# A written-out instruction order with a new tail: transformer block on one core, TensorE's groups reordered from the 167th on

## The chip, the core and the metric

The kernel runs on one core of one Trainium2 chip. The core has five engines that take instructions from queues of their own and wait for each other through semaphores: TensorE (PE in the profile; its weight loads are listed apart as PEld), VectorE (DVE), ScalarE (ACT), GpSimd (POOL) and SyncE (SP), which here only issues transfers. Transfers run on 16 DMA engines. The metric is the device time of one execution in microseconds (us), and one profiled execution gives the trace.

## The reference

The inputs are one sequence of 2048 tokens with 512 features (bfloat16), a condition vector and the weights. What has to come out is a transformer block whose two layer norms and two residual adds are modulated by the condition:

```python
mod = (silu(c) @ w_mod).reshape(1, 6, 1, -1)           # sa, ca, ga, sb, cb, gb
h = layernorm(x) * (1 + ca) + sa
x = x + ga * attention(h, wqkv, wo)     # 32 heads of 16; 8 keys: own position, -2, -4, ... -14
h = layernorm(x) * (1 + cb) + sb
x = x + gb * ((silu(h @ w1) * (h @ w3)) @ w2)          # 512 -> 1792 -> 512
```

A query sees its own position and the seven at distances 2 to 14 behind it, so attention has no square matrix: it is eight elementwise products of q with a shifted k, a softmax over eight numbers, and eight products with a shifted v.

## The kernel before

**Tiles and stages.** The 2048 tokens are 16 tiles T of 128 tokens. After layer norm 1, TensorE makes q, k and v (L691, L711). Per tile, VectorE multiplies q with eight shifted views of k in one instruction (L742, `pq`), and TensorE sums the products per head with a matrix of ones (L752, `lg`). The softmax runs on VectorE and ScalarE (L764 to L797, the exponential at L782), TensorE turns the weights (L807, `at`) and ScalarE copies them out (L811). Four transfers fetch eight shifted views of v for a tile (`vl`), VectorE multiplies them with the weights (L827, `av`), TensorE adds them up (L855, `ac`), ScalarE copies the sum to SBUF (L861), a transposing transfer turns it (L124, tile `ot`), TensorE multiplies with `wo` (L867, `wo`), and VectorE adds the result to x and takes its row sum (L871, `rs`).

**Layer norm 2.** For a pair of tiles GpSimd makes minus the mean from the two row sums (L586). ScalarE squares (L590, twice). GpSimd makes the reciprocal deviation and the bias in three small instructions (L596, L597, L599). ScalarE then normalises both tiles (L601). For the second group of tiles on, a transposing transfer per tile and four modulating ScalarE instructions (L621) make the `h` that the feed-forward part reads.

**Feed-forward part.** Tiles go through it in six groups: 0-1, 2-3, 4-7, 8-11, 12-13, 14-15. A group has 14 blocks of 128 hidden features. A block is four TensorE matmuls with w1 (the gate) and four with w3 (the up), both L883, 256 or 512 tokens wide. ScalarE takes the silu of the gate (L889), and VectorE multiplies it with the up (L892). The matmuls with w2 (L921, `z`) come in two halves of seven per tile, and VectorE adds x and the result is stored (L931).

**What sets the order.** No compiler orders anything here. `_build` makes 1118 operations with their dependencies; the list `ORDER` gives the sequence in which they are put into the queues of their engines, and `SLOTS` gives each pooled buffer its place (eight PSUM banks, six silu buffers, 20 product buffers and more). `synchronize` adds the waits that dependencies and buffer reuse need. An engine works through its queue strictly in order: an instruction that waits holds up all that stand behind it. A PE entry of the list is a group of matmuls, for example the four of one gate.

The numbers of `ORDER` that the text below uses:

- tiles 4 to 7: 470 is `ac` of tile 7, 471 its copy, 472 its transposing transfer, 473 its `wo`; 460 is `ac` of tile 6 and 459 its `av`; 746 is the gate of block 26, 733 a product of block 22; 484 is the last softmax step (L797) of tiles 8-9; 509 and 507 are `pq` of tiles 11 and 10; 767 is L599 of tiles 4-5 on GpSimd, 769 and 768 are the two L601 behind it; 773 to 775 are L596 to L599 of tiles 6-7; 717, 701, 719 and 721 are the products of blocks 18 and 14 and the silu and product of block 19; 753, 737 and 749 are products of blocks 27, 23 and 26; 501 and 491 are `av` of tiles 9 and 8
- tiles 8 to 11: 496 and 506 are `rs` of tiles 8 and 9, 858 is L586 of the two on GpSimd, 859 the first L590 behind it; 533 and 523 are `av` of tiles 11 and 10; 534 and 524 are their `ac`, 535 and 525 the copies; 833 and 821 are products of blocks 39 and 36
- tiles 12 to 15: 565 and 575 are `wo` of tiles 12 and 13, 566 and 576 their `rs`, 954 is L586 of the two, 956 and 955 the two L590; 586 and 596 are `av` of tiles 14 and 15, 587 and 597 their `ac`, 588 and 598 the copies, 590 and 600 their `wo`; 886 and 887 are gate and silu of block 43; 843, 847 and 851 are second halves of `z` (seven matmuls each)

Of the kernel before, what the change touches and what calls it, by code (L numbers as in the profile page):

```python
# [272 lines left out]
def _build(p, A_x, A_wqkv, A_wo, B_w1, B_w3, B_w2, c, w_mod, out):  # L273
# [722 lines left out]
    316, 444, 405, 406, 319, 617, 622, 626, 407, 446, 627, 395, 396, 397, 419, 420, 623, 477, 45, 634, 635, 447, 642, 618, 272, 320,  # L996
    46, 636, 637, 628, 629, 619, 620, 621, 52, 226, 326, 51, 630, 631, 408, 624, 625, 344, 638, 448, 421, 422, 50, 640, 639, 641,
    662, 670, 644, 643, 645, 449, 409, 646, 410, 450, 632, 647, 47, 633, 654, 398, 399, 451, 663, 666, 400, 671, 672, 452, 48, 343,
    650, 655, 668, 667, 669, 648, 649, 682, 683, 684, 453, 652, 651, 653, 435, 656, 657, 664, 433, 436, 685, 454, 665, 673, 658,
    678, 434, 437, 321, 426, 686, 687, 689, 695, 688, 694, 691, 660, 323, 659, 661, 423, 478, 475, 696, 424, 438, 425, 697, 690,  # L1000
    692, 674, 693, 742, 439, 730, 465, 731, 466, 468, 743, 427, 744, 745, 726, 706, 708, 707, 709, 476, 479, 467, 469, 428, 458,
    429, 710, 711, 456, 457, 712, 713, 722, 723, 724, 727, 728, 729, 455, 732, 733, 440, 725, 430, 746, 698, 699, 459, 53, 702, 703,
    480, 54, 470, 471, 472, 734, 735, 441, 442, 460, 461, 345, 346, 714, 431, 432, 738, 762, 462, 481, 497, 482, 473, 474, 483, 675,
    676, 747, 763, 463, 464, 704, 498, 484, 764, 765, 499, 715, 487, 716, 717, 700, 701, 718, 720, 509, 770, 771, 679, 705, 750,
    736, 737, 490, 748, 772, 485, 719, 500, 749, 488, 721, 739, 740, 752, 741, 507, 766, 767, 769, 489, 779, 768, 751, 754, 753,
    486, 501, 773, 774, 778, 775, 776, 780, 777, 781, 782, 491, 785, 758, 759, 760, 327, 783, 755, 529, 502, 510, 508, 492, 784,
    798, 818, 511, 512, 503, 531, 532, 680, 830, 493, 513, 330, 530, 831, 521, 539, 832, 514, 515, 820, 822, 814, 799, 815, 522,
    819, 504, 505, 516, 517, 541, 494, 324, 520, 495, 518, 506, 834, 806, 786, 807, 496, 761, 836, 794, 833, 823, 835, 677, 821,
    838, 858, 808, 859, 681, 533, 534, 559, 519, 523, 535, 809, 837, 540, 558, 542, 543, 524, 860, 525, 570, 790, 796, 795, 788,
    797, 545, 861, 791, 810, 787, 789, 802, 792, 793, 526, 544, 536, 547, 546, 549, 548, 862, 537, 569, 538, 550, 803, 527, 528,  # L1010
    839, 863, 864, 804, 805, 811, 551, 594, 812, 813, 866, 824, 825, 867, 800, 567, 593, 552, 553, 554, 874, 592, 868, 869, 826,
    557, 816, 560, 801, 840, 827, 870, 871, 555, 872, 568, 556, 817, 876, 841, 865, 854, 875, 561, 873, 846, 877, 828, 571, 842,
    595, 881, 562, 572, 829, 577, 563, 584, 855, 879, 578, 579, 564, 573, 850, 856, 580, 574, 878, 880, 906, 908, 581, 596, 565,
    566, 575, 576, 954, 857, 585, 907, 583, 909, 918, 919, 894, 582, 586, 843, 956, 955, 957, 886, 887, 958, 756, 898, 587, 588,
    895, 597, 890, 891, 589, 926, 847, 598, 599, 959, 960, 962, 899, 900, 901, 927, 961, 848, 590, 600, 591, 601, 1032, 910, 920,
    921, 963, 964, 965, 892, 893, 967, 966, 1034, 928, 1033, 1035, 1036, 1037, 851, 968, 852, 849, 972, 974, 976, 978, 973, 980,
    929, 911, 984, 986, 977, 979, 975, 844, 845, 985, 987, 853, 1039, 988, 990, 989, 1038, 930, 931, 932, 981, 982, 983, 933, 902,
    904, 991, 903, 905, 970, 934, 969, 1040, 896, 897, 971, 882, 1041, 888, 889, 884, 883, 922, 885, 923, 935, 936, 924, 946, 1043,
    1042, 942, 937, 938, 950, 1004, 1006, 1005, 1007, 1000, 1045, 1002, 1001, 925, 1008, 1012, 1009, 1013, 1016, 1017, 996, 998,
    997, 914, 999, 915, 1018, 992, 1003, 1044, 993, 994, 1014, 1015, 1019, 995, 916, 757, 912, 917, 1024, 913, 939, 1028, 940, 1070,  # L1020
    1090, 1071, 1086, 1072, 1073, 1091, 1010, 1087, 1074, 1011, 1082, 1075, 1088, 941, 1083, 1078, 1089, 1079, 1092, 1093, 1094,
    1084, 1096, 1095, 1097, 1080, 1081, 943, 951, 1085, 952, 944, 947, 948, 949, 1054, 1050, 1066, 1051, 1052, 1053, 953, 945, 1020,
    1062, 1064, 1076, 1077, 1063, 1046, 1067, 1068, 1069, 1047, 1055, 1056, 1057, 1021, 1022, 1023, 1058, 1060, 1059, 1061, 1029,
    1048, 1025, 1098, 1049, 1030, 1065, 1099, 1100, 1101, 1110, 1111, 1112, 1114, 1115, 1113, 1116, 1117, 1026, 1027, 1102, 1031,
    1103, 1104, 1105, 1106, 1107, 1108, 1109,
]
SLOTS = [
    7, 0, 1, 2, 3, 4, 5, 6, 0, 1, 2, 3, 4, 5, 6, 7, 0, 1, 2, 3, 4, 5, 6, 7, 0, 3, 4, 5, 6, 0, 1, 1, 0, 2, 3, 0, 4, 0, 7, 1, 0, 2, 1,
    2, 3, 6, 1, 5, 0, 7, 5, 7, 6, 2, 2, 1, 4, 0, 1, 3, 1, 2, 0, 4, 1, 4, 0, 7, 5, 1, 3, 6, 3, 0, 4, 2, 0, 1, 2, 1, 1, 0, 2, 4, 0, 1,
    2, 1, 4, 3, 6, 5, 1, 1, 0, 1, 3, 2, 3, 2, 4, 0, 0, 2, 3, 4, 1, 0, 3, 5, 6, 5, 1, 5, 3, 3, 2, 2, 0, 2, 6, 1, 2, 0, 3, 6, 7, 5, 3,  # L1030
    0, 1, 1, 0, 6, 0, 1, 1, 0, 0, 0, 0, 0, 1, 1, 5, 1, 6, 0, 1, 1, 1, 0, 5, 1, 0, 3, 1, 5, 0, 2, 3, 1, 4, 0, 2, 4, 2, 100, 5, 1, 2,
    5, 1, 1, 0, 1, 4, 0, 7, 1, 0, 4, 0, 1, 1, 1, 1, 5, 0, 7, 0, 0, 1, 1, 6, 0, 1, 1, 1, 0, 5, 1, 0, 0, 100, 7, 0, 2, 1, 1, 6, 0, 2,
    6, 2, 100, 5, 1, 1, 3, 1, 3, 0, 2, 5, 0, 4, 1, 0, 0, 1, 0, 1, 6, 0, 0, 6, 1, 0, 4, 1, 7, 0, 2, 6, 6, 1, 0, 0, 1, 1, 6, 100, 2,
    0, 0, 2, 1, 4, 7, 2, 1, 5, 103, 2, 102, 3, 101, 6, 103, 1, 100, 4, 101, 5, 104, 2, 106, 4, 102, 3, 100, 3, 105, 2, 104, 1, 102,
    4, 105, 1, 100, 3, 108, 5, 104, 2, 109, 4, 105, 7, 110, 5, 102, 7, 113, 5, 103, 6, 111, 2, 102, 6, 107, 6, 101, 1, 112, 0, 100,
    3, 102, 0, 3, 2, 0, 4, 4, 104, 0, 101, 1, 105, 1, 102, 1, 105, 7, 115, 1, 103, 4, 116, 7, 100, 2, 100, 5, 101, 7, 105, 7, 101,
    5, 119, 2, 102, 1, 117, 7, 100, 7, 118, 5, 103, 2, 103, 4, 100, 5, 106, 5, 104, 4, 114, 2, 102, 0, 104, 6, 104, 4, 107, 2, 101,
    0, 101, 2, 1, 4, 3, 1, 1, 105, 5, 113, 3, 100, 1, 100, 6, 101, 0, 112, 1, 103, 5, 115, 3, 101, 1, 101, 6, 100, 5, 110, 6, 100,
    7, 102, 0, 102, 1, 116, 4, 101, 5, 109, 3, 104, 6, 105, 3, 101, 5, 103, 0, 105, 7, 108, 4, 105, 0, 111, 7, 105, 7, 119, 1, 103,
    3, 100, 5, 102, 4, 103, 0, 1, 2, 4, 2, 3, 105, 5, 108, 6, 103, 7, 105, 6, 105, 4, 114, 4, 102, 1, 115, 7, 101, 4, 106, 7, 100,  # L1040
    4, 113, 7, 100, 0, 104, 7, 104, 1, 114, 1, 100, 4, 113, 7, 104, 0, 107, 6, 100, 1, 116, 0, 100, 3, 117, 0, 101, 3, 110, 2, 102,
    4, 109, 7, 100, 3, 102, 0, 101, 5, 103, 0, 3, 0, 6, 101, 0, 103, 2, 101, 0, 100, 4, 105, 5, 118, 2, 100, 1, 102, 3, 100, 7, 101,
    4, 105, 5, 112, 4, 103, 6, 108, 2, 100, 4, 119, 4, 103, 6, 104, 6, 101, 2, 111, 2, 105, 1, 100, 4, 102, 1, 105, 1, 101, 2, 106,
    3, 103, 0, 113, 2, 102, 6, 100, 1, 2, 1, 0, 102, 3, 116, 1, 103, 5, 118, 4, 104, 5, 110, 7, 100, 4, 114, 0, 101, 1, 117, 7, 105,
    7, 109, 4, 102, 4, 115, 7, 100, 5, 107, 7, 102, 1, 108, 4, 104, 7, 112, 7, 103, 1, 101, 1, 101, 4, 102, 1, 105, 4, 103, 5, 105,
    0, 100, 3, 101, 6, 103, 7, 101, 4, 103,
]


# [26 lines left out]
```

## Time and profile before

| | |
|---|---|
| three runs | 239.98, 240.88 and 242.07 us, median 240.88 |
| the profiled execution | 240.36 us, of which 238.6 us are the span of its instructions |
| TensorE | busy 232.2 us (97% of the span), 1806 matmuls |
| VectorE | busy 179.4 us (75%) |
| ScalarE | busy 138.3 us (58%) |
| GpSimd | busy 28.8 us (12%) |
| granted TensorE clock | 1.0 throughout |
| transfers | 38.85 MB |

How to read the views quoted below: the timeline has start, duration, engine, line, operation, tiles and count, and in brackets the idle time ahead of the instruction with what ended it. The chain of waits has start, duration and what ran, over the instructions that lead back from the last one. A matmul's duration is its latency; matmuls overlap, so their pace is read from starts. The table of stages has, for each stretch, its length and the busy time and count of each engine.

### The profile page before, as it was taken

How to read it: one execution, taken by the hardware profiler on the slowest of the kernel's cores; microseconds unless marked ns; L12 is line 12 of the kernel's file. 1: busy time of each engine (PE TensorE's matmuls, PEld its weight loads, DVE VectorE, ACT ScalarE, POOL GpSimd, SP SyncE). 2: the span in 40 equal slices, each digit the busy share in tenths (PEclk: the TensorE clock that was granted, in tenths of full speed). 3: DMA queues.
4: the chain of work that ended last, by engine and by line, in shares of the span. 5: the costliest groups of instructions: out<-in, count | busy, mean ns of one | idle time of the engine just before them, and what ended most of it. 6: DMA issues, size and time to landing. Idle time of an engine off the chain costs nothing.

```text
span 238.6 us, 4560 instructions
## 1 busy us (share of the span) xinstructions
PE 232.2 (97%) x1806; PEld 136.7 (57%) x1806; DVE 179.4 (75%) x279; ACT 138.3 (58%) x267; POOL 28.8 (12%) x66
## 2 busy tenths in 40 slices
PE   7999999999999998999999999999899999999995
PEld 4776554545688683664444444444375457485874
DVE  5699999999999999899999999690653403434433
ACT  2289587899978737776765594747553406040300
POOL 4434000013002000240003420020010000000000
PEclk9999999999999999999999999999999999999999
DMA  6999999999999996876972783634303000000202
GB/s 216 372 330 309 157 242 301 217 288 315 302 293 254 247 203 178 240 180 193 229 220 62 192 209 76 166 113 46 67 5 104 3 0 0 3 22 0 69 1 88
DMA packets 46317, 38.85 MB, mean 163 GB/s; under 512 B 21704, under 2 KB 37080, under 8 KB 46296
## 3 DMA queue, kind: packets, MB, share of 16 engines
q1 hardware_dynamic: 46288, 38.56, 65.1%
q8 instruction: 14, 0.23, 0.4%
q14 instruction: 7, 0.06, 0.1%
q10 hardware_dynamic: 8, 0.00, 0.0%
HBM read 29.62 MB, written 4.21 MB: 142 GB/s over the span
## 4 chain that ended last, share of the span: by engine, by line
PE 83%; DMA 8%; DVE 3%; SPq 3%; ACT 1%; issue 0%
PE pall L883 40%; PE pall L921 17%; PE pall L691 7%; PE pall L867 5%; DMA sb_x<-in_A_x_dram 5%; PE pall L711 4%; DMA sb_ot<-sb_ac 3%; PE pall L752 3%; SPq L124 3%; PE pall L855 3%; PE pall L909 3%; DVE sb_pq L742 2%; DVE sb_st L555 1%; PE pall L807 1%; DVE sb_xn L576 1%; ACT sb_ac L861 0%
## 5 line engine op out<-in xcount | busy, mean ns | idle before, releaser
L883 PE MATMUL pall<-sb_h,sb_w 128*128 128x256 bf16 (+1 forms) x672 | 102.6, 308 | 0.0
L883 PEld LDWEIGHTS pall<-sb_h,sb_w 128*128 128x128 bf16 x672 | 65.0, 98 | 35.7 <-issue 2.5
L889 ACT ACTIVATE sb_sg<-pall 128x256 bf16<-128x256 f32 (+1 forms) x84 | 35.6, 454 | 54.5 <-PE pall L883 53.4
L892 DVE TENSOR_TENSOR sb_hh<-sb_sg,pall 128x256 bf16<-128x256 bf16 (+1 forms) x84 | 40.0, 505 | 36.1 <-PE pall L883 34.0
L921 PE MATMUL pall<-sb_w,sb_hh 128*128 128x512 bf16 x196 | 44.9, 379 | 0.0
L742 DVE TENSOR_TENSOR sb_pq<-sb_q,sb_kT 128x4096 bf16<-128x4096 bf16 x16 | 36.3, 2282 | 0.0
L921 PEld LDWEIGHTS pall<-sb_w,sb_hh 128*128 128x128 bf16 x196 | 19.0, 98 | 21.6 <-DVE sb_hh L892 0.4
L691 PE MATMUL pall<-sb_h,sb_wqkv 128*128 128x512 bf16 (+1 forms) x160 | 31.0, 336 | 0.0
L827 DVE TENSOR_TENSOR sb_vsh<-sb_vsh,sb_al 128x4096 bf16<-128x4096 bf16 x12 | 27.2, 2284 | 0.5 <-DMA sb_vsh<-v_scratch_dram 0.5
L621 ACT ACTIVATE sb_h<-sb_h,sb_modc 128x512 bf16<-128x512 bf16 (+1 forms) x24 | 16.5, 743 | 9.1 <-DMA sb_h<-sb_xn 9.1
L691 PEld LDWEIGHTS pall<-sb_h,sb_wqkv 128*128 128x128 bf16 x160 | 14.7, 98 | 11.7 <-ACT sb_ac L861 0.4
L931 DVE TENSOR_TENSOR sb_o<-pall,sb_x 128x512 bf16<-128x512 f32 (+1 forms) x18 | 11.1, 628 | 10.9 <-PE pall L921 7.1
L867 PE MATMUL pall<-sb_wo,sb_ot 128*128 128x512 bf16 x64 | 16.0, 379 | 1.9 <-DMA sb_ot<-sb_ac 1.9
L711 PE MATMUL pall<-sb_wqkv,sb_h 128*128 128x512 bf16 x64 | 16.0, 379 | 0.0
L644 ACT ACTIVATE sb_h<-pall,sb_modc 128x256 bf16<-128x256 bf16 (+1 forms) x18 | 9.9, 611 | 7.9 <-DVE sb_modc L509 6.9
L586 POOL TENSOR_SCALAR sb_nm<-sb_sx 128x2 f32<-128x2 f32 x8 | 1.7, 218 | 105.3 <-DVE sb_x L871 105.3
L861 ACT ACTIVATE sb_ac<-pall 128x512 bf16<-128x512 f32 x16 | 9.5, 595 | 7.1 <-PE pall L855 6.9
L601 ACT ACTIVATE sb_xn<-sb_x,sb_nb,sb_rs 128x512 bf16<-128x512 bf16 x16 | 12.4, 807 | 0.7 <-POOL sb_nb L599 0.6
L871 DVE SCALAR_TENSOR_TENSOR sb_x<-pall,sb_x 128x512 bf16<-128x512 f32 x16 | 10.8, 686 | 2.2 <-PE pall L867 2.1
L590 ACT ACTIVATE sb_xn<-sb_x,sb_nm 128x512 bf16<-128x512 bf16 x16 | 11.4, 714 | 1.8 <-POOL sb_nm L586 1.8
L721 ACT ACTIVATE sb_v<-pall 128x512 bf16<-128x512 f32 x16 | 9.6, 605 | 2.8 <-PE pall L711 2.8
L555 DVE BATCH_NORM_STATS2 sb_st<-sb_x 128x6 f32<-128x512 bf16 x16 | 10.5, 679 | 0.7 <-DMA sb_x<-in_A_x_dram 0.6
(87 smaller groups left out, 209.5 us busy)
## 6 DMA issues: line engine op xcount, KB each, us to landing
sb_vsh<-v_scratch_dram SPq DMA_DIRECT2D x48, 256.0 KB, 5.2
sb_vshx<-v_scratch_dram SPq DMA_DIRECT2D x16, 256.0 KB, 4.4
sb_w<-in_B_w_dram SPq DMA_DIRECT2D x6, 512.0 KB, 7.6
sb_w<-in_B_w_dram SPq DMA_DIRECT2D x6, 384.0 KB, 4.2
v_scratch_dram<-sb_v SPq DMA_DIRECT2D x16, 128.0 KB, 6.1
out_dram<-sb_o SPq DMA_DIRECT2D x14, 128.0 KB, 1.8
sb_wqkv<-in_A_wqkv_dram SPq DMA_DIRECT2D x6, 256.0 KB, 6.3
sb_x<-in_A_x_dram SPq DMA_DIRECT2D x4, 256.0 KB, 6.5
```

Source lines behind the costliest of these rows:

```text
L555: o = p.op("dve", lambda e, T=T: e.bn_stats(st[:, T, :], x_sb[:, T, :]), 595, ("st", T), r=[vx[T]], w=[vs])
L601: p.op("act", lambda e, vn=vn, T=T: e.activation(vn.at[:], x_sb[:, T, :], ACT.Identity, bias=nb[:, T, :], scale=rs[:, NT + T, :]), c_act(5 ...
L621: return e.activation(vh.at[:, ft, 0:n * P], vh.at[:, ft, 0:n * P], ACT.Identity, bias=modc[:, 8 * which + ft:8 * which + ft + 1], scale=m ...
L691: ins = e.matmul(bank(vp)[:, j * n:(j + 1) * n], wqkv[:, t, col:col + P], vh.at[:, t, 0:n], start=(t == ORDER[0] and j == 0), stop=(t == O ...
L711: ins = e.matmul(bank(vp), vh.at[:, t, tt * P:(tt + 1) * P], wqkv[:, t, 2 * D:3 * D], start=(t == ORDER[0]), stop=(t == ORDER[-1]))
L742: return e.tensor_tensor(vp.at[:], in0, in1, ALU.mult)
L827: return e.tensor_tensor(v_w, v_w, a_w, ALU.mult)
L867: ins = e.matmul(bank(vy), vt.at[:, ft, :], wo[:, ft, :], start=(ft == 0), stop=(ft == KT - 1))
L883: ins = e.matmul(bank(vp)[:, 0:n], wt[:, t, fi * P:(fi + 1) * P], vh.at[:, t, 0:n], start=(t == 0), stop=(t == KT - 1))
L889: p.op("act", lambda e: e.activation(vt.at[:, 0:n], bank(vgp)[:, 0:n], ACT.Silu), c_act(n), k, r=[vgp], w=[vt], table="silu")
L892: p.op("dve", lambda e: e.tensor_tensor(vh_.at[:, 0:n], vt.at[:, 0:n], bank(vup)[:, 0:n], ALU.mult), c_dve(n), k, r=[vt, vup], w=[vh_])
L921: ins = e.matmul(bank(vz), vhh[fi].at[:, tt * P:(tt + 1) * P], w2[:, fi, :], start=(fi == 0), stop=(fi == NF - 1))
```

## The change

Only the two lists change. TensorE gets the same groups from its 167th on in another sequence, with the silus, products, copies and adds that belong to them; the buffers are assigned anew (314 of 655 places). The queues of GpSimd and of the transfers keep their order, apart from the order of the last output stores. No instruction is added or taken away. The rewritten part of `ORDER` begins so:

```diff
-    650, 655, 668, 667, 669, 648, 649, 682, 683, 684, 453, 652, 651, 653, 435, 656, 657, 664, 433, 436, 685, 454, 665, 673, 658,
-    678, 434, 437, 321, 426, 686, 687, 689, 695, 688, 694, 691, 660, 323, 659, 661, 423, 478, 475, 696, 424, 438, 425, 697, 690,
+    650, 655, 668, 667, 669, 648, 649, 682, 683, 684, 453, 652, 651, 653, 435, 656, 657, 664, 433, 436, 685, 454, 434, 321, 426,
+    423, 424, 425, 678, 658, 686, 687, 688, 690, 694, 689, 465, 466, 468, 691, 467, 665, 673, 437, 695, 323, 660, 478, 659, 661,
...
```

Sorted by engine, these are the places that the prediction speaks of (old line, then new line):

```
TensorE, 184th to 201st group
- 428 710 712 722 724 728 732 746 698 702 470 734 441 460 714 431 738 473
+ 730 726 734 710 724 712 728 732 702 470 441 714 698 460 746 431 738 473
VectorE, around `av` of tile 6 (459) and the products of blocks 14 to 27
- 729 733 725 459 480 442
+ 725 729 459 480 733 442
- 484 717 701 509 705 737 749 721 741 507 753 501 491
+ 484 509 717 705 701 741 721 507 753 737 749 501 491
ScalarE, same place
- 771 772 719 739 769 768 751 486 776 777
+ 771 772 739 769 768 719 776 777 751 486
VectorE, tiles 8 to 11
- 541 506 496 833 821 533 523
+ 541 833 506 533 821 496 523
ScalarE, same place
- 835 859 535 860 525 795
+ 835 859 535 860 795 525
VectorE, tiles 12 to 15
- 596 566 576 909 586 756
+ 596 576 909 566 586 756
ScalarE, same place
- 907 919 956 955 887 588 895 891 598 960
+ 907 956 955 887 588 598 960
TensorE, from the 272nd group
- 906 908 565 575 918 894 843 886 898 587 597 890 926 847 900 590 600 910
+ 898 851 575 906 908 565 843 886 926 587 597 847 928 890 892 590 922 900 600 924
```

The waits that the new lists give at three of these places: 524 (`ac` of tile 10) waits for 535, the copy of tile 11's sum, and for 523; 597 (`ac` of tile 15) waits for 887, the silu of block 43; 954 (GpSimd) waits for 566.

## The prediction

> **What bounds the kernel now.** I read the busy shares first, then the waits of TensorE alone, then the table of stages.
>
> ```profile
> PE 232.2 (97%) x1806; PEld 136.7 (57%) x1806; DVE 179.4 (75%) x279; ACT 138.3 (58%) x267; POOL 28.8 (12%) x66
> ...
> PE pall L867 <- DMA sb_ot<-sb_ac: 1.9, 2, 1.0
> ...
> 96.00:152.00 56.00, 56.00 (x405) 27.89 (x404) 54.34 (x68) 37.90 (x68) 9.99 (x15) 1.00 0.70 181
> ...
> 170.00:238.60 68.60, 65.99 (x445) 43.21 (x442) 25.85 (x54) 20.53 (x49) 1.30 (x4) 1.00 0.09 26
> ```
>
> PE is busy 97% of the span. Over the new part of the order (76 us to the end) it waits three times: twice for a turned tile `ot`, and once for an `av` (the row of 92.04 below). Between 96 and 152 us it never stops, but VectorE is busy 54.34 of those 56.00 us, so whatever VectorE delays there has no spare time to be made up in. The number of PE groups does not change; so the new order can win only those three waits, and lose only by new ones.
>
> The sizes of the two waits for `ot`, by the PE timeline and the chain of waits:
>
> ```profile
> 93.90 0.60 PE L883 MATMUL pall<-sb_h,sb_w 128*128 128x256 bf16 x4
> 95.54 1.02 PE L867 MATMUL pall<-sb_wo,sb_ot 128*128 128x512 bf16 x4 [1.04 <-DMA sb_ot<-sb_ac]
> ...
> 166.51 1.03 PE L867 MATMUL pall<-sb_wo,sb_ot 128*128 128x512 bf16 x4
> 168.35 1.04 PE L867 MATMUL pall<-sb_wo,sb_ot 128*128 128x512 bf16 x4 [0.81 <-DMA sb_ot<-sb_ac]
> ...
> 90.82 1.03 PE L867 MATMUL pall<-sb_wo,sb_ot 128*128 128x512 bf16 x4
> 92.04 0.61 PE L855 MATMUL pall<-sb_vsh,sb_ind 128*32 128x512 bf16 x8 [0.19 <-DVE sb_vsh L827]
> ...
> 91.12 4.29 DMA sb_ot<-sb_ac
> ...
> 98.08 0.86 PE pall L867 x4
> 98.94 2.18 PE pall L883 x20
> 101.12 1.51 PE pall L921 x7
> ```
>
> Matmuls overlap, so I count from start to start, as the chain does: four matmuls of 512 columns take 0.86, seven 1.51, and four of 256 take 2.18 / 5 = 0.44. Hence `wo` of tile 7 is late by 95.54 - 93.90 - 0.44 = 1.20, `wo` of tile 15 by 168.35 - 166.51 - 0.86 = 0.98, `ac` of tile 6 by 92.04 - 90.82 - 0.86 = 0.36. Together 2.54 us: the most that can be won.
>
> **The change part by part.** I went through the new order group by group and put each under the time that its releaser had in this trace. From 76.7 to 89 us groups only trade places and every releaser is early enough: 0 (0 to 0.2 lost).
>
> *Tiles 6 and 7 (89 to 96 us).* The gate 746 (0.44) moves behind `ac` of tile 6, and the product 733 behind `av` of tile 6. So `av` starts earlier, and of 0.36 about 0.07 is left; `ac` of tile 7 and the transfer 472 behind it come 0.44 earlier, issued at 90.68. When it lands is the question. The DMA view for 90.5 to 95.5 us (each digit 0.125 us) and the tile view of `sb_ot`:
>
> ```profile
> DMA  9999999999600029996700000000000059994000
> ...
> q8 instruction: 1, 0.02, 1.7%
> ...
> DMA to landing us min/median/max: 2.4/3.6/6.6
> ```
>
> Most of the transfer is over at 93.4 us (digit 24 on is 0), and nothing else runs until the next transfer; the landing is counted at 95.41, after one block of PE's own instructions went through a DMA engine (1.7% of 16 engines' 5 us is 1.3 us on one). I read the late landing as this block in front of one sixteenth of the transfer. PE fetches it by its place in its own program, which in the new order comes 0.25 to 0.5 us earlier, so it may meet the transfer again. End A: same landing time, 90.68 + 4.29 + 0.13 = 95.10, 0.44 gained. End B: the shortest landing, 90.68 + 2.4 = 93.1, no wait at all, and `wo` of tile 7 starts at 94.05, 1.49 gained.
>
> The Trainium skill, "Runtime: NRT & Kernel Launch", section "Instruction fetch mechanics", says that crossing a 16 KiB instruction boundary is mostly hidden. By that alone end B would hold; this trace shows a landing of 4.29 against a shortest of 2.4, so here the fetch is not hidden from a waiting transfer.
>
> *GpSimd behind VectorE.* The next three parts rest on one observation, GpSimd's timeline beside VectorE's:
>
> ```profile
> 100.72 0.20 POOL L599 TENSOR_TENSOR sb_nb<-sb_nm,sb_rs 128x2 f32<-128x2 f32 x1
> 101.62 1.58 POOL L596 TENSOR_SCALAR sb_rs<-sb_var 128x2 f32<-128x2 f32 x1 [0.70 <-ACT sb_xn L590]
> ...
> 122.20 0.22 POOL L586 TENSOR_SCALAR sb_nm<-sb_sx 128x2 f32<-128x2 f32 x1 [17.95 <-DVE sb_x L871]
> 129.06 2.10 POOL L596 TENSOR_SCALAR sb_rs<-sb_var 128x2 f32<-128x2 f32 x1 [6.64 <-ACT sb_xn L590]
> 131.24 0.70 POOL L597 TENSOR_TENSOR sb_rs<-sb_rs,sb_cst 128x2 f32<-128x2 f32 x1
> ```
>
> ```profile
> 100.20 0.74 DVE L892 TENSOR_TENSOR sb_hh<-sb_sg,pall 128x256 bf16<-128x256 bf16 x2
> 100.86 2.29 DVE L742 TENSOR_TENSOR sb_pq<-sb_q,sb_kT 128x4096 bf16<-128x4096 bf16 x1
> ...
> 122.02 0.08 DVE L871 DVE_READ_ACCUMULATOR sb_x<-pall,sb_x 128x1 f32 x1
> ...
> 125.42 2.29 DVE L827 TENSOR_TENSOR sb_vshx<-sb_vshx,sb_al 128x4096 bf16<-128x4096 bf16 x1
> 128.82 2.28 DVE L742 TENSOR_TENSOR sb_pq<-sb_q,sb_kT 128x4096 bf16<-128x4096 bf16 x1
> 131.62 2.28 DVE L742 TENSOR_TENSOR sb_pq<-sb_q,sb_kT 128x4096 bf16<-128x4096 bf16 x1
> ...
> 156.57 0.69 DVE L871 SCALAR_TENSOR_TENSOR sb_x<-pall,sb_x 128x512 bf16<-128x512 f32 x1
> ```
>
> The small GpSimd instruction that starts within a `pq` or `av` ends with it: 101.62 + 1.58 = 103.20 beside 100.86 + 2.29 = 103.15; 129.06 + 2.10 = 131.16 beside 128.82 + 2.28 = 131.10. One that starts ahead keeps its length: L599 at 100.72, 0.14 ahead of its `pq`, took 0.20; L597 at 131.24 took 0.70 and ran 0.32 into the `pq` of 131.62, which took 2.28 all the same.
>
> The Trainium skill, "SBUF — State Buffer", section "Who interferes with whom", has this as a rule: a VectorE instruction with two SBUF inputs contends with a GpSimd instruction that reads SBUF, and the one that issues first blocks the other for its whole length. The held GpSimd rows agree; the `pq` of 131.62, not lengthened, does not show the other half. By the full rule a `pq` behind a GpSimd start would lose at most 0.3 here.
>
> *Tiles 8 and 9's `av` (96 to 113 us).* `pq` of tile 11 stands directly behind 484, two products (100.20 to 100.86, 0.33 each) no longer ahead of it: it starts about 100.2, and 767 (the L599 of 100.72) falls inside it and ends near 102.4 instead of 100.92, 1.5 later. Behind 767 waits the L601 pair, and in the new order the silu 719 waits behind that pair:
>
> ```profile
> 101.44 0.63 ACT L889 ACTIVATE sb_sg<-pall 128x256 bf16<-128x256 f32 x2
> 101.97 1.51 ACT L601 ACTIVATE sb_xn<-sb_x,sb_nb,sb_rs 128x512 bf16<-128x512 bf16 x2
> 124.25 0.73 ACT L590 ACTIVATE sb_xn<-sb_x,sb_nm 128x512 bf16<-128x512 bf16 x1
> 127.68 0.60 ACT L861 ACTIVATE sb_ac<-pall 128x512 bf16<-128x512 f32 x1 [2.60 <-PE pall L855]
> 160.67 0.60 ACT L889 ACTIVATE sb_sg<-pall 128x512 bf16<-128x512 f32 x1 [1.24 <-PE pall L883]
> ...
> 104.88 6.21 PE L921 MATMUL pall<-sb_w,sb_hh 128*128 128x512 bf16 x28
> 128.36 0.61 PE L855 MATMUL pall<-sb_vshx,sb_ind 128*32 128x512 bf16 x8
> ...
> 156.36 1.89 PE L883 MATMUL pall<-sb_h,sb_w 128*128 128x512 bf16 x8
> 158.09 1.67 PE L921 MATMUL pall<-sb_w,sb_hh 128*128 128x512 bf16 x7
> 161.86 0.60 PE L855 MATMUL pall<-sb_vshx,sb_ind 128*32 128x512 bf16 x8
> ```
>
> Pair from 102.5 to 104.0, silu to 104.3 (two took 101.44 to 101.97), its product 721 to 104.75 with the handing over, `pq` of tile 10 to 106.95, three products to 107.95; then the third `z` of the 28, which before began at 104.88 + 2 x 1.51 = 107.90, can begin. In end A PE stood 0.44 ahead, and this uses it up. In end B the whole chain starts earlier with PE, and I estimate that 0.9 to 1.0 of the 1.49 stays. Call what is kept d: 0 to 1.0.
>
> *`ac` of tile 10 (120 to 130 us).* VectorE's six pieces ahead of `av` of tile 10 are the same (end 127.71 - d), but 496, the last row sum, now stands directly ahead of that `av`. The L586 of 122.20 needs it, so it starts inside the `av` and ends at 127.77 - d. Behind it is the L590 (0.71) at 127.82, and behind that the copy of tile 11's sum (0.60), until 129.13 - d. PE's `ac` of tile 10 waits for that copy: 129.2 - d against 128.36. With respect to before PE is then late by L = 0.85 - d. In end B that is below nothing.
>
> *`ac` of tile 15 (152 to 165 us).* The new order has a `z` half (1.51) where a group of 0.86 stood: +0.65 that comes back later. 565 is last ahead of the `z` that was at 158.09, which now begins at 158.74 + L. Its row sum 566 starts 0.21 behind the group's end, as the one of 156.57 did behind 156.36, and ends at 159.65 + L; `av` of tile 14 stands directly behind and takes until 161.86 + L; the L586 954 is held inside it to 161.92; two L590 follow (0.71 each, to 163.39), then the silu 887 (0.60, to 163.99), and `ac` of tile 15 waits for 887: 164.09 + L. PE would be there at 161.86 + 0.65 + L = 162.51 + L. A new wait of 1.58.
>
> *`wo` of tile 15.* Its 0.98 goes: two more groups stand ahead, and from `ac` of tile 15 to it are 7.2 us (one 1.51, six 0.86, 0.54). The two copies behind `ac` end near 165.4 + L; even with 4.29 the tile lands at 169.7 + L, and PE needs it at 171.3 + L. This cover ends only at a landing of 5.9.
>
> Behind 170 us VectorE is busy 25.85 of 68.60 us and ScalarE 20.53, so a silu or product that moves has room, and the tail of the list has the same dependencies: 0.
>
> Sum: L + 1.58 - 0.98 = 1.45 - d, with d from 0 to 1.0: **+0.45 to +1.45** on the profiled execution's 240.36, 240.8 to 241.8. That execution is 0.52 below the median of 240.88, so 241.3 to 242.3 as a median. I take the middle of d, since nothing in the trace tells where the block falls: +0.95, **241.8**.
>
> **The rivals.**
>
> *GpSimd is first (not slower).* The two held L586 are the price. In the trace L586 started at 122.20, 0.10 behind the end of the row sum's last piece (122.02 + 0.08); VectorE's pieces follow each other without a gap, so the hold should come; but if `av` loaded 0.2 us later, L586 would run in 0.22 as before, the copy would be at its old 127.7, and silu 887 done at about 161.9, ahead of PE. Then neither 0.85 nor 1.58 is paid and 0.98 + 0.44 to 0.98 + 1.49 is won: 237.9 to 238.9, or 238.4 to 239.5 as a median. For it speak the rows of 100.72 and 131.24, which were first by 0.14 and 0.38; against it, the order of the list. 0.14.
>
> *A second block of instructions on a transposition that PE waits for (slower).* The page has 14 such blocks of PE in 238.6 us, one per 17 us. `wo` of tile 8 now goes before that of tile 9, and the last transpositions of the layer norm stand closer to their groups. The price is 4.29 - 2.4 = 1.9, of which the two new waits could cover some: 1.0 to 1.9, 241.8 to 243.3 on the profile's base, 242.3 to 243.8 as a median. It decides if a block begins within the 2.4 us of a transfer that has under 1.9 us to spare: 2.4 / 17 = 0.14 for each. 0.16.
>
> ```profile
> q8 instruction: 14, 0.23, 0.4%
> ```
>
> *Only names move.* If releasers were early everywhere (no hold, no late copy, no better `ot`), the time would stay at 240.9. VectorE's 54.34 of 56.00 us speaks against it. 0.08.
>
> **How the numbers follow.** Forecast 0.56, the rivals 0.14, 0.16 and 0.08, 0.06 for what I don't see. 1%, about what a measurement of this kernel can tell from no change, is 238.47 to 243.29. Faster by more: the lower edge of the first rival and half of the unseen, 0.06. Slower by more: the upper third of the second and some of the unseen, 0.10. The rest, 0.84, is within. The range from 239.3 to 243.3 holds the forecast, the third rival and most of the second; it leaves out nearly all of the first.
>
> **What would show it.** Right: the GpSimd row of L586 near 125 and 160 us lasts about 2.2 us instead of 0.22; PE waits at L855 near 128 and 163 us, released by ScalarE; no wait of PE at L867 near 171 us; L599 near 100 us lasts over 1.5 us. The wait at L867 near 95 us gives d. Wrong: short L586 rows with no wait at L855 (then the first rival), a landing above 4 us ahead of other `wo` (the second), or a wait behind 170 us, which I have at nothing.

## The result, and the profile after

The changed kernel takes 241.72 us (median of 22 runs) and the kernel before 240.00 us (median of 22 runs, the three shown above among them). The ratio is 1.0084, 95% interval 1.0061 to 1.0107: slower by 0.8%, clear of the noise, and of a size that the prediction put within 1%. Two slow runs of the changed kernel (247.72 and 851.74 us) are left out of the ratio, and the two medians alone give 1.0072. The profiled execution took 241.0 us with a span of 239.3, so the two traces differ by 0.7 us only, the medians by 1.7. That gap is part of what had to be explained.

The waits of PE behind 76 us, changed kernel (what PE waited for, us in total, times, longest), where before had the two `ot` and an `av`:

```profile
PE pall L855 <- ACT sb_sg L889: 1.3, 1, 1.3
PE pall L855 <- ACT sb_ac L861: 0.8, 1, 0.8
```

The three old waits are gone and two new ones stand at `ac`. Some matmul records are missing in this trace (1779 of 1806), so I read starts and not sums. The PE timeline around the places that the prediction named (start, duration, idle time ahead in brackets):

```profile
94.48 1.03 PE L867 MATMUL pall<-sb_wo,sb_ot 128*128 128x512 bf16 x4
...
126.69 1.06 PE L752 MATMUL pall<-sb_pq,sb_E 128*32 128x256 bf16 x32
128.58 0.61 PE L855 MATMUL pall<-sb_vshx,sb_ind 128*32 128x512 bf16 x8 [0.84 <-ACT sb_ac L861]
...
162.30 0.61 PE L855 MATMUL pall<-sb_vsh,sb_ind 128*32 128x512 bf16 x8
164.23 0.62 PE L855 MATMUL pall<-sb_vshx,sb_ind 128*32 128x512 bf16 x8 [1.32 <-ACT sb_sg L889]
...
171.48 1.03 PE L867 MATMUL pall<-sb_wo,sb_ot 128*128 128x512 bf16 x4
```

`wo` of tile 7 comes at 94.48 (95.54 before) and `wo` of tile 15 at 171.48, both without a wait; `ac` of tile 10 is 0.98 late by pace: before, it started 0.91 behind the `lg` ahead of it (127.45 and 128.36), and 126.69 + 0.91 = 127.60. `ac` of tile 15 is 1.49 late: before, it started 0.44 behind the `ac` of tile 14 (161.42 and 161.86), and 162.30 + 0.44 = 162.74. Why they are late stands in the chain of waits of the changed kernel (start, duration, what ran):

```profile
125.01 2.20 POOL sb_nm L586
127.21 0.02 issue
127.23 0.81 ACT sb_xn L590 x2
128.05 0.49 ACT sb_ac L861
128.54 0.04 issue
128.58 0.61 PE pall L855 x8
...
159.96 2.20 POOL sb_nm L586
162.16 0.02 issue
162.18 1.52 ACT sb_xn L590 x4
163.70 0.49 ACT sb_sg L889
164.19 0.04 issue
164.23 0.62 PE pall L855 x8
```

A GpSimd instruction of 0.22 us (122.20 and 157.35 before) is now a 2.20 us piece of the path, twice. VectorE's timeline shows beside what it ran:

```profile
124.84 0.08 DVE L871 DVE_READ_ACCUMULATOR sb_x<-pall,sb_x 128x1 f32 x1
124.84 2.29 DVE L827 TENSOR_TENSOR sb_vshx<-sb_vshx,sb_al 128x4096 bf16<-128x4096 bf16 x1
...
159.78 2.29 DVE L827 TENSOR_TENSOR sb_vsh<-sb_vsh,sb_al 128x4096 bf16<-128x4096 bf16 x1
```

L586 starts 0.17 and 0.18 behind the start of the `av` and ends 0.08 and 0.09 behind its end (125.01 + 2.20 = 127.21 beside 124.84 + 2.29 = 127.13). The L599 near 100 us went the same way:

```profile
99.78 1.81 POOL L599 TENSOR_TENSOR sb_nb<-sb_nm,sb_rs 128x2 f32<-128x2 f32 x1
```

### The profile page after: what moved, and what is told of

Same layout as the page of the kernel before. It is cut to its first block, busy times and chain, and to the rows that moved or that the text cites. A ratio compares the mean times of both kernels' runs of the same rounds, so it can differ in the third digit from the quotient of the medians.

```text
span 239.3 us, 4531 instructions
## 1 busy us (share of the span) xinstructions
PE 230.3 (96%) x1779; PEld 136.1 (57%) x1806; DVE 179.3 (75%) x279; ACT 137.8 (58%) x267; POOL 29.4 (12%) x66
## 4 chain that ended last, share of the span: by engine, by line
PE 54%; DVE 17%; DMA 10%; SPq 6%; ACT 5%; POOL 4%; issue 3%
PE pall L883 25%; PE pall L921 12%; SPq L124 6%; DMA sb_x<-in_A_x_dram 5%; DMA sb_vsh<-v_scratch_dram 5%; DVE sb_pq L742 4%; PE pall L691 4%; PE pall L711 3%; DVE sb_vsh L827 3%; PE pall L909 3%; PE pall L867 3%; DVE sb_x L871 2%; POOL sb_nm L586 2%; PE pall L752 2%; PE pall L855 2%
## 5 line engine op out<-in xcount | busy, mean ns | idle before, releaser
L921 PE MATMUL pall<-sb_w,sb_hh 128*128 128x512 bf16 x186 | 44.3, 379 | 0.6 <-issue 0.2
L691 PE MATMUL pall<-sb_h,sb_wqkv 128*128 128x512 bf16 (+1 forms) x154 | 30.2, 335 | 0.5 <-issue 0.2
L586 POOL TENSOR_SCALAR sb_nm<-sb_sx 128x2 f32<-128x2 f32 x8 | 5.7, 711 | 113.5 <-DVE sb_x L871 113.4
L590 ACT ACTIVATE sb_xn<-sb_x,sb_nm 128x512 bf16<-128x512 bf16 x16 | 11.4, 713 | 7.8 <-POOL sb_nm L586 7.7
L711 PE MATMUL pall<-sb_wqkv,sb_h 128*128 128x512 bf16 x62 | 15.5, 379 | 0.2
```

The costliest lines, as they stand in the source:

```text
L691: ins = e.matmul(bank(vp)[:, j * n:(j + 1) * n], wqkv[:, t, col:col + P], vh.at[:, t, 0:n], start=(t == ORDER[0] and j == 0), stop=(t == O ...
L711: ins = e.matmul(bank(vp), vh.at[:, t, tt * P:(tt + 1) * P], wqkv[:, t, 2 * D:3 * D], start=(t == ORDER[0]), stop=(t == ORDER[-1]))
L921: ins = e.matmul(bank(vz), vhh[fi].at[:, tt * P:(tt + 1) * P], w2[:, fi, :], start=(fi == 0), stop=(fi == NF - 1))
```

## The experiments

Each changed order is the new order with a few entries moved; `ORDER.remove(op)` and an insertion behind the second number do it, and the pairs are shown. Ratios are to the kernel before, with 95% intervals. To compare places in the traces I use the start of a PE group's first weight load, counted from that of the 166th group, the last that is common: what happens in the first 76 us then drops out.

### Each consequence taken away alone

The copy ahead of the first L590 on ScalarE:

```diff
+for op, behind in ((859, 535),):
+    ORDER.remove(op)
+    ORDER.insert(ORDER.index(behind) + 1, op)
```

> The changed kernel with the first L590 of tiles 8-9 (859) behind the copy of tile 11's sum (535) on ScalarE. Theory (the held L586 delays the L590, the L590 delays the copy, the copy delays PE): the L586 row near 125 us still lasts 2.2 us, the copy no longer waits, the wait at L855 near 128 us goes from 0.98 to under 0.1, and all behind is 0.9 to 1.0 earlier: 0.8 to 1.0 us faster than the changed kernel, ratio to before 1.004. Rival (the wait is av of tile 10, which PE needs as well and which ends at 127.13): the wait stays above 0.5.

Measured: 241.94 us, ratio 1.0069 [1.0037, 1.0101], against 241.75 and 1.0073 [1.0041, 1.0105] for the changed kernel measured beside it: no gain to be seen in the times. The trace shows the local effect, and where it went. GpSimd, PE and VectorE timelines, copy first:

```profile
126.47 2.19 POOL L586 TENSOR_SCALAR sb_nm<-sb_sx 128x2 f32<-128x2 f32 x1 [22.09 <-DVE sb_x L871]
130.46 1.58 POOL L596 TENSOR_SCALAR sb_rs<-sb_var 128x2 f32<-128x2 f32 x1 [1.79 <-ACT sb_xn L590]
...
132.90 1.94 POOL L599 TENSOR_TENSOR sb_nb<-sb_nm,sb_rs 128x2 f32<-128x2 f32 x1
```

```profile
129.03 0.61 PE L855 MATMUL pall<-sb_vshx,sb_ind 128*32 128x512 bf16 x8
...
154.02 1.04 PE L883 MATMUL pall<-sb_h,sb_w 128*128 128x512 bf16 x4 [0.27 <-ACT sb_h L621]
```

```profile
87.56 2.29 DVE L827 TENSOR_TENSOR sb_vsh<-sb_vsh,sb_al 128x4096 bf16<-128x4096 bf16 x1 [1.34 <-DMA sb_vsh<-v_scratch_dram]
```

L586 is held as before, and `ac` of tile 10 no longer waits, so the path over the copy is right and the `av` is not what PE waits for. But the rest of the layer norm of tiles 8 and 9 now falls into the next two `pq`: L596 and L599 take 1.58 and 1.94 (in the changed kernel's first trace 1.26 and 0.20), and PE waits 0.27 at 154.02 for the modulated tiles. From `ac` of tile 10 to the 272nd group it is 24.98 instead of 24.50. The traced execution also had late transfers ahead of tile 7 (the row of 87.56; more of them further down). A gain of 0.5, which is what the trace leaves, is no larger than what the interval can tell; the expected 0.8 to 1.0 is not confirmed by the times.

The silu ahead of the two L590:

```diff
+for op, behind in ((956, 887), (955, 956)):
```

> The changed kernel with the two L590 of tiles 12-13 (956, 955) behind the silu of block 43 (887) on ScalarE. Theory: L586 near 160 us still lasts 2.2 us, the silu runs at 161.4 instead of 163.6, the wait at L855 near 164 us goes from 1.49 to under 0.1, the turned tiles 14 and 15 come up to 0.2 later or earlier without a wait at L867: 1.3 to 1.6 us faster than the changed kernel, ratio to before 1.002. Rival (PE then waits for the modulated tiles of the next group, whose L590 is now later, near 177 us): under 0.7 faster.

Measured: 240.47 us, ratio 1.0024 [0.9999, 1.0049], 1.3 us below the changed kernel. GpSimd and PE:

```profile
160.76 2.19 POOL L586 TENSOR_SCALAR sb_nm<-sb_sx 128x2 f32<-128x2 f32 x1 [17.86 <-DVE sb_x L871]
```

```profile
95.38 1.02 PE L867 MATMUL pall<-sb_wo,sb_ot 128*128 128x512 bf16 x4 [1.03 <-DMA sb_ot<-sb_ac]
...
129.39 0.61 PE L855 MATMUL pall<-sb_vshx,sb_ind 128*32 128x512 bf16 x8 [0.35 <-ACT sb_ac L861]
...
163.54 0.60 PE L855 MATMUL pall<-sb_vshx,sb_ind 128*32 128x512 bf16 x8
...
179.25 2.01 PE L883 MATMUL pall<-sb_h,sb_w 128*128 128x512 bf16 x9 [0.53 <-ACT sb_sg L889]
```

The wait at 164 us is gone with L586 still held, so it came over the L590 in front of the silu. In this trace PE then waits 0.53 at 179.25 for a silu behind the next layer norm, so a part comes back, much as the rival had it, but the times keep 1.3 of the 1.3 to 1.6 that the theory gave. It also shows the block of instructions on the transfer of tile 7 (1.03 at 95.38; the transfer lands after 4.5 us), and behind it the wait of `ac` of tile 10 at 0.35 instead of 0.84: what PE loses ahead of that place, it waits less there.

### The cause taken away

```diff
+for op, behind in ((821, 496), (533, 821), (909, 566)):
```

> The changed kernel with a product between the row sum and the av on VectorE at both places (821 behind 496, av of tile 11 behind 821; 909 behind 566), ScalarE's order untouched. Theory (an L586 that starts inside an av is held until its end, one that starts inside a product is not): both L586 rows last 0.22 us; no wait at L855 near 128 us; near 163 us PE waits 0.3 to 0.5 for av of tile 14, which starts 0.6 later, instead of 1.49: 1.7 to 2.1 us faster than the changed kernel, ratio to before 1.000 to 1.002. Rival (L586 is slow for another reason, such as its own wait): the rows stay near 2.2 us and the time within 0.5 us of the changed kernel.

Measured: 239.99 us, ratio 1.0011 [0.9984, 1.0038], 1.8 us below the changed kernel, within what the theory gave. GpSimd, VectorE and PE:

```profile
123.09 0.22 POOL L586 TENSOR_SCALAR sb_nm<-sb_sx 128x2 f32<-128x2 f32 x1 [19.29 <-DVE sb_x L871]
...
159.98 0.22 POOL L586 TENSOR_SCALAR sb_nm<-sb_sx 128x2 f32<-128x2 f32 x1 [17.77 <-DVE sb_x L871]
```

```profile
122.92 0.68 DVE L892 TENSOR_TENSOR sb_hh<-sb_sg,pall 128x512 bf16<-128x512 bf16 x1
123.52 2.28 DVE L827 TENSOR_TENSOR sb_vsh<-sb_vsh,sb_al 128x4096 bf16<-128x4096 bf16 x1
...
159.81 0.68 DVE L892 TENSOR_TENSOR sb_hh<-sb_sg,pall 128x512 bf16<-128x512 bf16 x1
```

```profile
162.75 0.61 PE L855 MATMUL pall<-sb_vsh,sb_ind 128*32 128x512 bf16 x8 [0.36 <-DVE sb_vsh L827]
```

Inside a product, which reads one operand from SBUF and one from PSUM (`sb_sg,pall`), L586 takes 0.22; inside an `av`, which reads both from SBUF, 2.19. That is the hold, shown at both places by putting one product of VectorE between the row sum and the `av`. Behind 120 us only the 0.36 for the later `av` of tile 14 remains; near 95 us this trace has a wait of 1.00 for `ot` of tile 7, whose transfer took 4.4. The Trainium skill, "SBUF — State Buffer", section "Who interferes with whom", says that a VectorE instruction with at most one SBUF input does not contend with GpSimd, outside certain fast modes; the row of 123.09 agrees.

Both places mended, the second by ScalarE's order:

```diff
+for op, behind in ((821, 496), (533, 821), (956, 887), (955, 956)):
```

> The changed kernel with both causes taken away: 821 and av of tile 11 behind the row sum 496 on VectorE (as in the run with the rows apart), and the two L590 956 and 955 behind the silu 887 on ScalarE. Theory: L586 near 123 us lasts 0.22, no wait at L855 anywhere behind 120 us, 2.2 to 2.5 us faster than the changed kernel, ratio to before 0.997 to 0.999. Rival (the waits were only the place where an older delay showed; it turns up later): within 1 us of the changed kernel, ratio above 1.003.

Measured: 240.02 us, ratio 1.0010 [0.9982, 1.0038]. No wait at L855 behind 120 us, but 1.7 us below the changed kernel by the medians (1.5 by the ratios, since the two were measured at different times) instead of the 2.2 to 2.5 of the theory. The trace shows a part given back, PE's timeline:

```profile
119.17 1.02 PE L867 MATMUL pall<-sb_wo,sb_ot 128*128 128x512 bf16 x4 [0.28 <-ACT sb_sg L889]
...
153.49 1.04 PE L883 MATMUL pall<-sb_h,sb_w 128*128 128x512 bf16 x3 [0.21 <-ACT sb_h L621]
```

A silu and a modulated tile are late where PE now comes earlier, and in this execution v of tile 7 was late too (VectorE waits 1.02 for it), so one trace does not split the shortfall. Counted from the 166th group, the last group starts at 159.29 here and at 158.61 in the trace with the rows apart, against 159.05 for before and 160.51 for the changed kernel (means of two and four traces, table further down).

And with the hold of L599 near 100 us kept off the silu as well:

```diff
+for op, behind in ((769, 719), (768, 769), (779, 768), (778, 779), (821, 496), (533, 821), (956, 887), (955, 956)):
```

> The kernel with both causes taken away, and also the silu of block 19 (719) ahead of the two L601 (769, 768) on ScalarE, so that it does not wait behind the held L599 of tiles 4-5. Theory: L599 near 100 us still lasts about 1.8 us, the silu runs about 1 us earlier, pq of tile 10 starts 0.6 earlier, and 0.3 to 0.4 of PE's waiting between 100 and 111 us goes: 0.3 us faster than with two causes mended, ratio to before 0.996 to 0.999. Rival (what is gained there is taken back at tiles 8 to 11): ratio as with two causes mended, 1.001.

Measured: 241.01 us, ratio 1.0041 [1.0006, 1.0075]. GpSimd and PE:

```profile
101.61 1.77 POOL L599 TENSOR_TENSOR sb_nb<-sb_nm,sb_rs 128x2 f32<-128x2 f32 x1
```

```profile
114.35 5.99 PE L883 MATMUL pall<-sb_h,sb_w 128*128 128x512 bf16 x27 [0.60 <-ACT sb_h L621]
121.62 1.02 PE L867 MATMUL pall<-sb_wo,sb_ot 128*128 128x512 bf16 x4 [1.28 <-DMA sb_ot<-sb_ac]
```

L599 is held as foreseen, and from `wo` of tile 7 to `ac` of tile 9 it is 15.58 us instead of 15.87 with two causes mended: the 0.3 is won there. It is lost again directly behind, at 0.60 and 1.28 for transposed tiles, as the rival had it. Why the times come out 1 us above the version with two causes mended stays open; the intervals overlap, and the trace doesn't show it. The traced execution took 242.34 us, but it reaches the 166th group at 78.39 us instead of 75.89, with a granted clock of 0.91 in its first 20 us, and from there to the last group it needs 158.97, less than the 159.29 with two. No order tried here beats the one before.

### The halves of the change

The old order up to the 271st PE group and the new behind it, and the other way round, with 25 and 13 buffers placed anew to fit (in short form):

```diff
-ORDER = [...]
+ORDER = old[:850] + new[850:]        # and new[:850] + old[850:]
```

> The order of before up to PE's 271st group (152.9 us), the new order behind it (25 buffers given other places so that the two parts fit): the part of the change at tiles 12 to 15 alone. Theory: L586 near 160 us held (2.2 us), PE waits about 1.5 at L855 near 164 us and not at L867 near 171 us, the end 0.5 later than in the first trace of before; in the median, where before does not always lose its 0.98, 0.5 to 1.2 later: ratio 1.002 to 1.005. Rival (the loss lies at tiles 8 to 11 and in the transfers ahead of them): ratio 0.998 to 1.001.

> The new order up to PE's 271st group (152.9 us), the order of before behind it (13 buffers given other places): the part of the change at tiles 6 to 11 alone. Theory: L586 near 125 us held, a wait of 0.3 to 1.0 at L855 near 128 us, L586 near 157 us 0.22, wo of tile 15 waits 0.4 to 1.0 at L867; 0.1 to 0.9 later than before at the 271st group and no more behind it: ratio 1.001 to 1.005. Rival (all of the loss is at tiles 12 to 15): ratio 0.997 to 1.000.

Measured: 1.0103 [1.0063, 1.0143] and 1.0104 [1.0071, 1.0137], both outside what the theory gave. Each half alone costs as much as the whole, so the totals can't be added. Each has waits that neither kernel has, PE of the first and the second:

```profile
175.96 4.28 PE L883 MATMUL pall<-sb_h,sb_w 128*128 128x512 bf16 x18 [0.91 <-ACT sb_sg L889]
```

```profile
158.90 1.04 PE L883 MATMUL pall<-sb_h,sb_w 128*128 128x512 bf16 x4 [0.35 <-DVE sb_hh L892]
...
162.52 1.04 PE L883 MATMUL pall<-sb_h,sb_w 128*128 128x512 bf16 x4 [0.21 <-DVE sb_o L931]
...
170.13 1.04 PE L867 MATMUL pall<-sb_wo,sb_ot 128*128 128x512 bf16 x4 [0.52 <-DVE sb_o L931]
```

Whether the other buffers or the seam cause them wasn't settled. The local steps are as in the whole: the new second half has the 1.32 at `ac` of tile 15, the new first half 0.50 at `ac` of tile 10.

### Why traces and medians differ

> The changed kernel unchanged. Its first trace ends only 0.7 us behind that of before (spans 239.3 and 238.6), but its median is 1.7 us behind. If chance decides whether the block of PE's instructions meets the transfer of tile 7 (it came at 93.15, the transfer ended at 93.34), a second trace has a fair chance to show PE waiting at L867 near 95 us for about 1.1 us, with a span near 240.4; the waits at L855 near 128 and 164 us (0.98 and 1.49 from start to start) stay within 0.2 either way. If the blocks play no part, the second trace shows the same waits as the first and the 1 us between trace and median stays unexplained. Time against before: 1.006 to 1.011 in both cases.

> The changed kernel unchanged, a third trace. Two of its traces show av of tile 7 waiting about 0.5 for its v and wo of tile 7 18.1 us behind the 166th group; the trace with the copy moved shows 1.3 and 19.35. Theory (the 12 times in the run before last fell into two heaps, 240.7 to 241.2 and 242.3 to 242.8, by how late the transfers ahead of tile 7 end): if this execution takes 242 us or more, wo of tile 7 comes over 19 us behind the 166th group; if it takes under 241.3, under 18.5. Rival: no relation.

> The changed kernel unchanged, a fourth trace, for the same question as the third: at 242 us or more wo of tile 7 comes over 19 us behind the 166th group, under 241.3 us it comes under 18.5 behind it; the rival sees no relation.

> The kernel before, unchanged: how far two measurements of one kernel differ (ratio 1.000, within 0.3%), and a second trace of it. Theory (its two waits at L867, 1.20 near 95 us and 0.98 near 168 us, come from a block of PE's instructions that meets a transfer by chance): the second trace lacks one of them or has it smaller by over 0.4. Rival (the two transfers are slow for a reason that is always there): both waits again within 0.2.

Measured: 241.75 us (1.0073 [1.0041, 1.0105]) for the changed kernel again, 0.9994 [0.9964, 1.0024] for the kernel before against itself; the third and fourth traces took 243.68 and 242.38 us. The second trace of the changed kernel has the same waits as the first, so the block on tile 7's transfer, which was expected to show there, didn't. The second trace of before lacks the wait for `ot` of tile 7 and has 0.57 instead of 0.98 for that of tile 15, as expected. Starts of the first weight load, counted from that of the 166th PE group, us. For `ac` of 15 it is the first matmul, because in the two traces of before the weight load runs 0.21 ahead of it and in the changed kernel the two start together:

| trace | time | `wo` of 7 | `ac` of 9 | `ac` of 10 | 272nd group | `ac` of 15 | last group |
|---|---|---|---|---|---|---|---|
| before | 240.36 | 19.39 | 34.90 | 52.24 | 76.74 | 85.75 | 159.17 |
| before again | 240.04 | 19.46 | 35.04 | 52.39 | 76.89 | 85.90 | 158.92 |
| changed | 241.00 | 18.18 | 34.06 | 52.39 | 76.89 | 88.04 | 159.85 |
| changed, second | 241.24 | 18.11 | 34.15 | 52.49 | 77.00 | 88.14 | 159.95 |
| changed, third | 243.68 | 18.66 | 35.15 | 53.48 | 77.98 | 89.13 | 160.94 |
| changed, fourth | 242.38 | 19.30 | 35.18 | 53.51 | 78.06 | 89.17 | 161.31 |

The fourth trace is as expected (over 242, 19.30). The third isn't (18.66). It lost 1.6 us ahead of the 166th group already, which it reaches at 77.78 us instead of 76.19, and the table of stages of the first and the third trace shows where (the third number from the end is the granted TensorE clock):

```profile
0.00:20.00 20.00, 17.93 (x174) 13.26 (x177) 14.83 (x49) 10.40 (x19) 8.26 (x29) 1.00 0.97 302
...
0.00:20.00 20.00, 16.91 (x149) 12.02 (x151) 13.79 (x45) 8.28 (x15) 7.20 (x26) 0.91 0.96 303
```

A clock of 0.91 over 20 us is 1.8 us of full clock missing, about what was lost. Another 0.5 is lost up to `wo` of tile 7 and 0.6 behind it. So the two heaps of times have more than one cause. What the fourth lost shows in VectorE's and PE's timelines:

```profile
87.16 2.29 DVE L827 TENSOR_TENSOR sb_vsh<-sb_vsh,sb_al 128x4096 bf16<-128x4096 bf16 x1 [1.29 <-DMA sb_vsh<-v_scratch_dram]
```

```profile
89.84 0.61 PE L883 MATMUL pall<-sb_h,sb_w 128*128 128x256 bf16 x4 [0.85 <-DVE sb_hh L892]
...
91.57 0.81 PE L867 MATMUL pall<-sb_wo,sb_ot 128*128 128x512 bf16 x3 [0.57 <-DMA sb_ot<-sb_ac]
```

The transfers ahead of tile 7 end 0.7 later in that execution than in the first trace, and what should be won at tiles 6 and 7 is gone. The kernel before reaches `wo` of tile 7 at 19.4 in either of its traces, by two different ways: in the first the late transfer of `ot`, in the second late v and an `ot` in time:

```profile
87.22 2.29 DVE L827 TENSOR_TENSOR sb_vsh<-sb_vsh,sb_al 128x4096 bf16<-128x4096 bf16 x1 [1.16 <-DMA sb_vsh<-v_scratch_dram]
```

So before loses this microsecond in both, and the changed kernel wins it in two traces of four. The mean of the last column is 159.05 for before and 160.51 for the changed kernel: 1.5 later, near the 1.7 of the medians, where the first two traces had shown 0.7. Two and four traces are few, and how often each case comes up is not shown.

### The blocks of instructions

```diff
+            if i < 16:
+                e.matmul(bank(vw)[:, 0:P], ones[:, 0:P], ones[:, 0:P], start=True, stop=True)
+                return e.matmul(bank(vw)[:, P:256], ones[:, 0:P], ones[:, P:256], start=True, stop=True)
             return e.matmul(bank(vw)[:, 0:256], ones[:, 0:P], ones[:], start=True, stop=True)
```

> The kernel before with 16 of the 24 warm-up matmuls at the start split into two of half the width: the same columns, 16 matmuls more, so every block of PE's instructions is fetched 16 matmuls earlier in the program, about 90.5 instead of 92.98 and 162.5 instead of 165.9. Theory (the blocks make the transfers of tiles 7 and 15 late): both transfers land within 2.6 us of their issue, no wait at L867 near 95 or 168 us, 0.7 to 2.0 us faster than before, ratio 0.992 to 0.997. Rival (something else delays them): landings and time as before, ratio 1.000.

Measured: 241.43 us, ratio 1.0040 [1.0007, 1.0072]: slower, against both expectations. PE's timeline and the chain of waits (lines are 3 higher here):

```profile
115.34 5.99 PE L886 MATMUL pall<-sb_h,sb_w 128*128 128x512 bf16 x27 [1.63 <-ACT sb_h L624]
```

```profile
107.54 4.57 DMA sb_h<-sb_xn
112.11 0.02 issue
112.13 2.94 ACT sb_h L624 x4
```

The wait for `ot` of tile 15 did go, but the block near 93 us still meets the transfer of tile 7 (3.8 us, PE waits 0.37), and another block now meets the transposition of a modulated tile, which takes 4.57 instead of 2.4 (the tile view of before has 2.4 to 2.7 for that pair), and PE waits 1.63. From `ac` of tile 9 to that of tile 10 it is 18.68 instead of 17.34, and from there to the last group 106.05 instead of 106.93 and 106.53: one wait is won and a longer one paid. So the blocks do delay transpositions that they meet, and moving them all moves the cost to another. The 16 matmuls more are not the price: the 166th group starts at 76.34 us instead of 76.12 and 76.01. The blocks also came less early than worked out (93.62 and 164.61 instead of 90.5 and 162.5, in an execution with late v). This is the second rival's mechanism, in the kernel before.

## Why the prediction was right, and where its sizes were off

- **Time.** 241.8 was forecast and 241.72 measured, within the range. That is partly luck: the three runs that stood for before had a median of 240.88 and the 22 have 240.00, 0.88 lower, and the step was forecast as +0.95 and measured as +1.7. Two errors of nearly one size cancel.
- **GpSimd behind VectorE.** Right in all three places: L586 2.19 and 2.19, L599 1.81, and the hold goes when the VectorE instruction is another one. The first rival (GpSimd gets in first) fell: L586 starts 0.17 behind the `av` in the traces; the third (only names move) fell with the two new waits.
- **`ac` of tile 10.** Forecast L = 0.85 - d, with d what PE had in hand. In the four traces the way from `ac` of tile 9 to that of tile 10 is 18.33, 18.34, 18.33 and 18.33, against 17.34 and 17.35: 0.99 longer every time. The mechanism held, and the term was 0.14 too small.
- **d.** Forecast 0 to 1.0, taken as 0.5. By `ac` of tile 9 in the table against the first trace of before: 0.84, 0.75, -0.25 and -0.28, mean 0.27, and two of the four lie outside the bounds. The step that failed is "tiles 6 and 7": I bounded it by the landing of `ot` alone and took the earlier transfers as they stood in one trace; in the changed order `ac` and `wo` hang on these as well. In all four traces the block misses the transfer of tile 7, which lands after 2.4 us (end B), and still the 1.49 of end B at its `wo` was 1.21 in the first trace and 0.09 in the fourth. The part "tiles 8 and 9's `av`" was right that a lead shrinks there: from 1.21 at `wo` of tile 7 to 0.84.
- **`ac` of tile 15.** Forecast +0.65 that comes back and a wait of 1.58; from the 272nd group it is 11.15 instead of 9.01, so 0.65 and 1.49, the same as by pace in the first trace. The term was 0.09 too large.
- **`wo` of tile 15.** Forecast 0.98 won. From `ac` of tile 15 to the last group it is 71.81 (three traces) and 72.14 instead of 73.42 and 73.02; with 71.81 and less the 0.65 that comes back, 0.96 is won against the first trace of before and 0.56 against the second, where the wait was only 0.57. On the mean of all traces it is 0.7. The term was right for the trace it was read from; the old wait was not the same in every execution.
- **Behind 170 us.** No wait of PE in the changed kernel, as forecast.
- **The second rival** (a block on another transposition) didn't show in the changed kernel's waits. Its first half did happen: in all four traces a block meets the transposition of a modulated tile near 170 us, which then takes 3.8 to 4.6 us instead of 2.4, but PE has other work until it lands. With the blocks moved in the kernel before, PE did wait.

The sum with the measured terms is 0.99 + 1.49 - 0.27 - 0.7 = +1.5, the 1.5 of the table. That is bookkeeping from the same traces; what shows the cause is the run with the rows apart.

## What to carry to other kernels

A short instruction on a side engine can become the path when the instruction beside it changes: look not only at which engine waits for which, but at what each small instruction will run next to. An order that frees an engine ahead of a fixed stop wins nothing if the stop doesn't move; follow the lead to the next place where the engine must wait. And a wait that is read from one trace is a sample: take the trace of the same kernel twice before counting its disappearance as a gain.

## What the runs showed of the hardware that I had not expected

- A block of PE's own instructions that meets a transposing transfer makes it land up to 2.2 us later: 4.3 to 4.5 us instead of 2.3 to 2.5 for `ot` of tile 7 (four traces with, nine without, and 3.8 with a block in the fourteenth), 3.7 and 3.3 for `ot` of tile 15 in the two traces of before against 2.4 in the changed kernel, 4.57 instead of 2.4 for the modulated tile above. At the very end of a transfer it cost nothing: in the first trace of the changed kernel the block begins at 93.15 us, and the transfer ends at 93.34, after 2.4. The Trainium skill, "Runtime: NRT & Kernel Launch", section "Instruction fetch mechanics", calls the crossing mostly hidden; for PE's own issue no wait shows, but for a transfer in flight it isn't hidden.
- The end of a backlog of transfers differs by 1.7 us between executions with the same transfers in the same order: v of tile 7, which VectorE waits for, lands between 85.8 and 87.5 us, those executions left out that had lost over 1 us by the 166th group. Within one kernel it was 86.0 and 87.2 in the two traces of before.
- In two of the fourteen traces, the third of the changed kernel and the one with three places mended, the granted clock is 0.91 in the first 20 us instead of 1.00, and the 166th group starts at 77.78 and 78.39 us instead of 75.7 to 76.5.
